# Attention products as pairs of 64-row matmuls, with separate accumulators for the two halves

## The chip, the cores and the metric

The kernel runs on one core of a Trainium2 chip. The metric is device microseconds from launch to end. TensorE (PE in the profile) multiplies, with its weight loads on a row of their own (PEld); VectorE (DVE) and ScalarE (ACT) do the elementwise work; SyncE (SP) issues the DMAs.

## What is computed

```python
scores = (1 / S) * z @ z.T            # per batch; S = 3008, z is S x 64
attn = maximum(scores, 0) ** 2
x = u * (attn @ v)                    # u, v: S x 256, two batches
h = x @ w_in                          # 256 -> 2048
x = (h - tanh(h)) @ w_out             # 2048 -> 256
out = (sigmoid(x @ w_gate) * (x @ w_val)) @ w2_out   # 256 -> 1536 -> 256
```

The reference works on two batches of 3008 tokens, attention first, then the two feed-forward networks (FFNs) on all 6016 tokens. The FFN weights are float64.

## The kernel before

A float32 operand is split into hi and lo, float32r numbers of 12 significant bits, and a product is made of three passes: hi x hi, lo x hi, hi x lo, summed in PSUM. Everything is transposed: features on partitions, tokens along the free dimension, in 12 chunks of queries, six per batch: five of 512 tokens and one of 448.

Attention takes a chunk's keys in 12 units of two 128-key tiles. `front` makes the scores of both tiles into one PSUM tile `s` of two banks (pool `psf`, two such tiles). A z tile holds hi and lo twice, so that 128 partitions are filled: its first plane is hi over lo, its second lo over hi. With the first plane as weights, the product with the first plane of the queries gives hi x hi + lo x lo, that with the second hi x lo + lo x hi: two matmuls of 128 rows for a tile, four for a unit, with a fourth product, lo x lo, among them. `mid1` is Relu and Square on ScalarE, CAST to `ah` and subtraction to `al` on VectorE. `back`, two units later, multiplies v into two accumulators, one for each 128 features (`acc0`, `acc1`): three passes, two tiles, two features, 12 matmuls. In a chunk's last unit the second key tile has only 64 keys; they stand in it twice, so that hi and lo of the scores share one pass: 10 matmuls. `end` comes one unit after the last `back` (`LATE`): two multiplies by u on VectorE, and a DMA to `spill`.

Accumulators come from the pool `psa`: tags `acc0` and `acc1` with two banks each, so four banks. A chunk takes one of each tag, and the next chunk the other.

The order of everything is written out by hand. The last loop goes over units n; in each it emits the steps in `todo` (loads, splits of z and v, one step of the float64 weights' decoding, which goes on all through attention), then `front` and `mid1` of unit n, `mid2` of unit n-1, a pending `end`, and `back` of unit n-2 (for attention). Each engine runs its own instructions in that order, and semaphores tie the engines together. The first FFN joins in the last attention chunk; until then attention has TensorE to itself.

Of the kernel before, what the change touches and what calls it, by code (L numbers as in the profile page):

```python
# [7 lines left out]
F32 = mybir.dt.float32  # L8
F32R = mybir.dt.float32r
U32 = mybir.dt.uint32  # L10
I64 = mybir.dt.int64
AF = mybir.ActivationFunctionType
ALU = mybir.AluOpType

P = 128
NQ = 512

# h - tanh(h) = tanh(h) * (GAMMA * tanh(BETA * h))^2 to 2e-6 for |h| below 0.28, where
# the square passes SQUARE_MAX; past it the difference itself is as good, and is taken.
BETA = 0.3157513921594212  # L20
GAMMA = 1.8284945624500233
SQUARE_MAX = 0.0259977

# A float64 is read as two uint32 words. Its high word, seen as a float32 and scaled by 2^-48, has the
# exponent of the wanted float32 three bits too low; these are the bounds where that exponent is in range.
WORD_MIN = 2.0**-63
WORD_MAX = 1.875 * 2.0**-32

# [2 lines left out]
def squared_relu_attention__then__two_ffns(  # L31
# [9 lines left out]
    w2_out: bass.AP,  # L41
    outT: bass.AP,
):
    """Float32 products run as float32r passes: x = hi + lo exactly, hi and lo of 12 significant
    bits each, and a @ b = a_hi b_hi + a_hi b_lo + a_lo b_hi, summed in float32 in PSUM.

    Everything is transposed: features on partitions, tokens (chunks of up to 512) along the free
    dimension. The float64 weights come as int64 and are decoded to float32 while attention runs."""
    nc = tc.nc
    B, S, D = v.shape  # L50
    DQ = zT.shape[1] // 2
    FF1 = w_in.shape[1]
    FF2 = w2_gate.shape[1]
    ND = D // P
    KT = -(-S // P)
    KP = KT // 2
    NZ = -(-S // NQ)
    HALF = S - (KT - 1) * P
    SCALE = 1.0 / S
    assert HALF * 2 == P and ND == 2 and DQ * 2 == P and KT % 4 == 0  # L60
    LATE = 1  # units from a chunk's last back to the emptying of its accumulators
    START = 2.5  # the unit of the last attention chunk after which the FFNs come in
    LAG = 5  # units that the second FFN stays behind the end of the first
    W2_LAG = 16  # units from the first FFN's start to the first split of the second's weights

    ring = ctx.enter_context(tc.tile_pool(name="ring", bufs=42))
    work = ctx.enter_context(tc.tile_pool(name="work", bufs=9))
# [1 line left out]
    psf = ctx.enter_context(tc.tile_pool(name="psf", bufs=2, space=bass.MemoryType.PSUM))  # L69
    psa = ctx.enter_context(tc.tile_pool(name="psa", bufs=2, space=bass.MemoryType.PSUM))  # L70
# [10 lines left out]
    z_t, v_t, u_t, x_t, y_t, w_t, w32 = {}, {}, {}, {}, {}, {}, {}  # L81

    chunks = []
# [3 lines left out]
    NC = len(chunks)  # L87
    spill = [nc.dram_tensor(f"x_{c}", (P, ND, chunks[c][3]), F32, kind="Internal").ap() for c in range(NC)]

# [1 line left out]
    def z_steps(b, j):  # L91
        box = []

# [37 lines left out]
        return load, lambda: split(0), lambda: split(1)  # L131

    def w_steps(src, key, g, rows):
        """Two tiles of 128 x 512 weights: float64 words to float32, kept in one slot."""
        raw, t = [], []

        def load():
            for i in range(2):
                r = slot([2, 256], I64, f"raw_{key}{g}_{i}")
                if rows:  # L140
                    s = src[(2 * g + i) * 2 * P : (2 * g + i + 1) * 2 * P]
                else:
                    s = src[:, (2 * g + i) * 256 : (2 * g + i + 1) * 256]
                nc.sync.dma_start(out=r, in_=s.rearrange("(t p) d -> p t d", p=P))
                raw.append(r)

        def words(i, h):
            return raw[i].rearrange("p t f -> p (t f)").bitcast(U32).rearrange("p (n two) -> p n two", two=2)[:, :, h]

        def magnitude():  # L150
            w = slot([2, 512], F32, f"{key}{g}_32")
            s = slot([2, 512], U32, f"{key}{g}_s")
            t.extend((w, s))
            for i in range(2):
                nc.scalar.activation(w[:, i], words(i, 1).bitcast(F32), AF.Abs, scale=2.0**-48)
            nc.vector.tensor_scalar(w, w, WORD_MAX, WORD_MIN, ALU.min, ALU.max)

        def sign():
            for i in range(2):
                nc.vector.tensor_scalar(t[1][:, i], words(i, 1), 0x80000000, None, ALU.bitwise_and)  # L160

        def join():
            w, s = t[0].bitcast(U32), t[1]
            nc.vector.scalar_tensor_tensor(
                out=w, in0=w, scalar=3, in1=s, op0=ALU.logical_shift_left, op1=ALU.bitwise_or
            )
            nc.vector.tensor_scalar(s, w, 0xFF800000, None, ALU.bitwise_and)

        def rest(i):
            s = t[1][:, i].bitcast(F32)  # L170
            nc.vector.scalar_tensor_tensor(
                out=s, in0=words(i, 0), scalar=2.0**-52, in1=s, op0=ALU.mult, op1=ALU.mult
            )

        def add():
            w, s = t[0], t[1].bitcast(F32)
            nc.vector.tensor_tensor(out=w, in0=w, in1=s, op=ALU.add)
            w32[key, g] = w

        def split(i):  # L180
            w = w32[key, g][:, i].rearrange("p (t f) -> p t f", t=2)
            r = slot([2, 2, 256], F32R, f"{key}{2 * g + i}")
            nc.scalar.copy(r[:, 0], w)
            sub(r[:, 1], w, r[:, 0])
            w_t[key, 2 * g + i] = r

        return (load, magnitude, sign, join, lambda: rest(0), lambda: rest(1), add), (
            lambda: split(0),
            lambda: split(1),
        )  # L190
# [19 lines left out]
        sub(lo[:, :, :n], x[:, :, :n], hi[:, :, :n])  # L210
        x_t[c] = (hi, lo)

# [1 line left out]
    class Unit:  # L214
        def accumulate(self, acc, wt, hl, w, first, last):
            n = self.n
# [25 lines left out]
    class Attention(Unit):  # L242
        kind, ahead = 0, 2
# [40 lines left out]
        def end(self, acc):  # L284
            u, n = u_t[self.c], self.n
            for d in range(ND):
                nc.vector.tensor_tensor(out=u[:, d, :n], in0=acc[d][:, :n], in1=u[:, d, :n], op=ALU.mult)  # L287
            nc.sync.dma_start(out=spill[self.c], in_=u[:, :, :n])

    class Ffn1(Unit):  # L290
        kind, ahead = 1, 3
# [50 lines left out]
    class Ffn2(Unit):  # L342
        kind, ahead = 2, 3
# [34 lines left out]
                copy(o[:, d, :n], acc[d][:, :n])  # L378
                nc.sync.dma_start(out=outT[d * P : (d + 1) * P, self.t0 : self.t0 + n], in_=o[:, d, :n])

# [1 line left out]
    N1, N2 = FF1 // P // 2, FF2 // P  # L382
    units = [Attention(c, i) for c in range(NC - 1) for i in range(KP)]
    n_att = len(units)
    mixed = [(i, 0, Attention(NC - 1, i)) for i in range(KP)]
    mixed += [(START + f, 1, Ffn1(0, f)) for f in range(N1)]
    mixed += [(KP + (c - 1) * N2 + f * N2 / N1, 1, Ffn1(c, f)) for c in range(1, NC) for f in range(N1)]
    mixed += [(KP + c * N2 + f + LAG, 2, Ffn2(c, f)) for c in range(NC) for f in range(N2)]
    units += [t[2] for t in sorted(mixed, key=lambda t: t[:2])]
    start, where = {}, {}  # L390
# [7 lines left out]
    def at(n, fn):  # L398
        todo.setdefault(max(n, 0), []).append(fn)

    # z and v: those of the first batch as early as it goes, those of the second while the first runs out
    for b in range(B):
        zs = [z_steps(b, j) for j in range(NZ)]
        vs = [v_steps(b, j) for j in range(NZ)]
# [1 line left out]
        if b == 0:  # L406
            early = [-2] * NZ
        else:
            early = [-2 - 2 * (NZ - j) for j in range(NZ)]
# [7 lines left out]
        for j in range(NZ):  # L417
            n = need[j] + early[j]
# [3 lines left out]
    for c in range(NC):  # L422
        at(start[0, c] + 2, lambda c=c: load_u(c))
        n = start[1, c]
# [7 lines left out]
    n = 8  # L432
    half = start[0, NZ]
    split = {}
    for k, p in enumerate(parts):
# [5 lines left out]
        if half - 14 < n < half + 4:  # L441
            n = half + 4
    for f in range(N1):
        n = where[1, 0, f]
        at(n - 3, split["wi1_", f // 2][f % 2])
        at(n - 2, split["wo1_", f // 2][f % 2])
    for f in range(N2 // 2):
        n = where[1, 0, 0] + W2_LAG + 2 * f
        assert n < where[2, 0, 2 * f]
# [6 lines left out]
    with tc.manual_schedule():  # L456
        nc.vector.memset(square_max, -SQUARE_MAX)
        nc.scalar.activation(warm, square_max, AF.Tanh)
        accs = {}
        backs = {}  # L460
        for n, u in enumerate(units):
            backs.setdefault(n + u.ahead, []).append(u)
        pending = []
        total = len(units)
        for n in range(total + 8):
            for fn in todo.pop(n, ()):
                fn()
            if n < total:
                units[n].front()
                units[n].mid1()  # L470
            if 0 <= n - 1 < total:
                units[n - 1].mid2()
            if pending and n >= pending[0][0]:
                _, u, a = pending.pop(0)
                u.end(a)
            for u in backs.pop(n, ()):
                if u.first:
                    accs[u.kind] = [psa.tile([P, NQ], F32, tag=f"acc{d}", name=f"acc{d}") for d in range(ND)]
                u.back(accs[u.kind])
                if u.last:  # L480
                    pending.append((n + LATE, u, accs[u.kind]))
        assert not todo and not pending


# ---- launch: one core; u and z transposed, z twice and its last half tile of keys repeated, the float64 weights as int64,
# the result transposed ----
# [24 lines left out]
```

## Time and profile before

| | |
|---|---|
| Three runs | 1617.8, 1619.4, 1619.55 us, median 1619.4 |
| Profiled execution, span from first to last instruction | 1618.1 us |
| PE busy, 7176 matmuls | 1605.8 us (99%) |
| PEld busy, 7176 loads | 1350.2 us (83%) |
| DVE busy | 1108.7 us (69%) |
| ACT busy | 1033.8 us (64%) |
| Attention alone on TensorE | until about 476 us |

The page gives the profiled execution by its span alone; the times of the runs are of other executions. Busy shares are means over stages. A matmul's record lasts longer than the time by which it delays the next one, so matmuls are priced by the distance of their starts. A weight load belongs to the matmul after it and runs beside the one before.

### The profile page before, as it was taken

What the parts mean: (1) busy time and instruction counts of PE and PEld (TensorE: products, weight loads), DVE (VectorE), ACT (ScalarE), POOL (GpSimd) and SP (SyncE); (2) the same over time, 40 slices, a digit from 0 to 9 for tenths busy, and PEclk for the clock granted to TensorE, in tenths of its full rate; (3) what the DMA queues carried; (4) which work ended last, traced back from release to release, by engine and by line L of the source; (5) the groups of instructions that cost most, each with busy time, mean ns of one, the idle gap of its engine ahead of it and who ended that gap; (6) DMA issues with size and microseconds to landing.
All of it is one profiled execution on the core that took longest, in us unless ns stands there. A gap on an engine that the chain in (4) does not pass through costs nothing.

```text
span 1618.1 us, 17871 instructions
## 1 busy us (share of the span) xinstructions
PE 1605.8 (99%) x7176; PEld 1350.2 (83%) x7176; DVE 1108.7 (69%) x1278; ACT 1033.8 (64%) x1232; POOL 0.2 (0%) x4
## 2 busy tenths in 40 slices
PE   8999999999999999999999999999999999999999
PEld 6888888888888878888888888888888888888888
DVE  7988888888868987665665656666565656565642
ACT  8666677666668886656665656666666656665532
POOL 0000000000000000000000000000000000000000
PEclk9999999999999999999999999999999999999999
DMA  6222214111110000000000000000000000000000
GB/s 221 79 79 78 72 52 135 61 52 62 48 38 27 1 25 0 1 27 0 27 1 25 1 27 1 0 27 1 25 1 27 1 26 1 1 25 1 13 1 25
DMA packets 28147, 53.05 MB, mean 33 GB/s; under 512 B 1952, under 2 KB 10144, under 8 KB 28064
## 3 DMA queue, kind: packets, MB, share of 16 engines
q1 hardware_dynamic: 28064, 51.91, 9.4%
q8 instruction: 56, 0.92, 0.2%
q14 instruction: 27, 0.22, 0.0%
HBM read 39.58 MB, written 12.32 MB: 32 GB/s over the span
## 4 chain that ended last, share of the span: by engine, by line
PE 98%; DVE 1%; DMA 0%; ACT 0%; issue 0%; SPq 0%; DVEq 0%
PE acc L223 51%; PE gv L235 24%; PE h L235 16%; PE s L257 8%; DMA vraw<-v 0%; DVE e L79 0%; DVE th L316 0%; DVE th L315 0%; DVE yl L79 0%; DVE u L287 0%; ACT a L263 0%; ACT th L310 0%; ACT sq L311 0%; SPq L96 0%; DVE gl L79 0%
## 5 line engine op out<-in xcount | busy, mean ns | idle before, releaser
L79 DVE TENSOR_TENSOR e<-h,th 128x1024 f32<-128x1024 f32 (+1 forms) x96 | 115.4, 1202 | 286.9 <-ACT sq L311 286.9
L223 PE MATMUL acc<-ah,v 128*128 128x512 f32 (+1 forms) x1104 | 292.5, 387 | 0.0
L223 PEld LDWEIGHTS acc<-ah,v 128*128 128x128 f32 x1104 | 208.3, 189 | 39.7 <-DVE ah L268 0.5
L263 ACT ACTIVATE a<-s 128x1024 f32<-128x1024 f32 (+1 forms) x144 | 145.5, 1010 | 149.4 <-PE s L257 149.2
L310 ACT ACTIVATE th<-h 128x1024 f32<-128x1024 f32 (+1 forms) x96 | 97.0, 1010 | 218.2 <-PE h L235 218.2
L235 PE MATMUL h<-xh,wi 128*128 128x512 f32 (+1 forms) x768 | 234.0, 386 | 1.2 <-DVE e L79 1.2
L223 PE MATMUL acc<-p,wo 128*128 128x512 f32 (+1 forms) x864 | 215.5, 386 | 0.0
L223 PE MATMUL acc<-gh,wo 128*128 128x512 f32 (+1 forms) x768 | 204.9, 386 | 0.5 <-DVE yl L79 0.4
L223 PEld LDWEIGHTS acc<-p,wo 128*128 128x128 f32 x864 | 162.3, 188 | 29.9
L79 DVE TENSOR_TENSOR al<-a,ah 128x1024 fp32r<-128x1024 f32 (+3 forms) x156 | 175.2, 1123 | 15.2 <-DVE ah L268 0.5
L360 ACT ACTIVATE sg<-gv 128x512 f32<-128x512 f32 (+1 forms) x144 | 84.5, 587 | 157.1 <-PE gv L235 157.1
L223 PE MATMUL acc<-al,v 128*128 128x512 f32 (+1 forms) x600 | 179.0, 386 | 0.0
L235 PE MATMUL gv<-yh,wg 128*128 128x512 f32 (+1 forms) x576 | 175.4, 386 | 0.0
L235 PE MATMUL gv<-yh,wv 128*128 128x512 f32 (+1 forms) x576 | 175.2, 385 | 0.0
L361 DVE TENSOR_TENSOR sg<-gv,sg 128x512 f32<-128x512 f32 (+1 forms) x144 | 98.3, 683 | 106.4 <-ACT sg L360 106.4
L235 PEld LDWEIGHTS h<-xh,wi 128*128 128x128 f32 x768 | 144.2, 188 | 28.4 <-DVE e L79 1.6
L223 PEld LDWEIGHTS acc<-gh,wo 128*128 128x128 f32 x768 | 144.2, 188 | 28.0 <-DVE yl L79 1.2
L264 ACT ACTIVATE a<-a 128x1024 f32<-128x1024 f32 (+1 forms) x144 | 150.3, 1044 | 4.6
L235 PE MATMUL h<-xl,wi 128*128 128x512 f32 (+1 forms) x384 | 148.1, 386 | 0.0
L316 DVE COPY_PREDICATED th<-m,e 128x1024 f32<-128x1024 uint32 (+1 forms) x96 | 131.6, 1371 | 9.9
L223 PEld LDWEIGHTS acc<-al,v 128*128 128x128 f32 x600 | 113.0, 188 | 21.2
L257 PE MATMUL s<-z,z 128*128 128x512 f32 (+1 forms) x480 | 127.5, 388 | 1.8 <-ACT a L263 1.8
(81 smaller groups left out, 2184.0 us busy)
## 6 DMA issues: line engine op xcount, KB each, us to landing
raw_wo<-w_out SPq DMA_DIRECT2D x14, 512.0 KB, 5.8
vraw<-v SPq DMA_DIRECT2D x10, 512.0 KB, 6.9
u<-uT SPq DMA_DIRECT2D x10, 512.0 KB, 6.7
x<-u SPq DMA_DIRECT2D x10, 512.0 KB, 3.0
xl<-x SPq DMA_DIRECT2D x10, 512.0 KB, 3.8
outT<-o SPq DMA_DIRECT2D x20, 256.0 KB, 2.1
raw_wi<-w_in SPq DMA_DIRECT2D x8, 512.0 KB, 8.1
zraw<-zT SPq DMA_DIRECT2D x12, 256.0 KB, 5.9
```

The costliest lines, as they stand in the source:

```text
L79: nc.vector.tensor_tensor(out=out, in0=a, in1=b, op=ALU.subtract)
L223: nc.tensor.matmul(acc[d][:, :n], wt[:, wi, w, d * P : (d + 1) * P], hl[ai], start=first and m == 0, stop=last and m == len(passes) - 1,)
L235: nc.tensor.matmul(ps, w[:, wi, d, fi * P : (fi + 1) * P], xs[xi][:, d, :n], start=m == 0, stop=m == len(passes) - 1)
L257: nc.tensor.matmul(self.ps[:, e, :n], k, z_t[b, self.j][:, h, :n], start=h == 0, stop=h == 1)
L263: nc.scalar.activation(s, self.ps[:, :, :n], AF.Relu, scale=SCALE)
L264: nc.scalar.activation(s, s, AF.Square)
L310: nc.scalar.activation(t, h, AF.Tanh)
L316: nc.vector.copy_predicated(t, m.bitcast(U32), e)
L360: nc.scalar.activation(s[:, :n], self.ps[:, 0, :n], AF.Sigmoid)
L361: nc.vector.tensor_tensor(out=s[:, :n], in0=self.ps[:, 1, :n], in1=s[:, :n], op=ALU.mult)
```

## The change

The first 11 chunks use a new unit, `HalfAttention`; the twelfth keeps `Attention`. Every matmul of the new unit has only 64 rows of weights and of moving data, either partitions 0 to 63 or 64 to 127, and instructions alternate between the two. In `front` the upper and lower half make the scores of the two key tiles, each with three passes and without lo x lo: six matmuls of 64 rows. In `back` each product over 128 keys is cut into its two halves of 64, which sum into accumulators of their own: 24 matmuls, 18 in the last unit. A chunk thus holds four accumulator banks. `end` follows at once after the last `back`: for each feature half ScalarE copies the second half's accumulator to SBUF, and VectorE adds the first half's to it; then one multiply by u. In a chunk's first and last unit the products are sorted by feature. Comments are removed, and nothing else is different.

```diff
+    class HalfAttention(Attention):
+        def front(self):
+            b, n = self.b, self.n
+            self.ps = psf.tile([P, 2, NQ], F32, tag="f", name="s")
+            q = z_t[b, self.j]
+            for m, (ki, qi) in enumerate(((0, 0), (1, 0), (0, 1))):
+                for e in range(2):
+                    i = 2 * self.i + e
+                    r, c = slice(e * DQ, (e + 1) * DQ), (i % 4) * P
+                    nc.tensor.matmul(
+                        self.ps[:, e, :n], z_t[b, i // 4][r, ki ^ e, c : c + P], q[r, qi ^ e, :n], start=m == 0, stop=m == 2
+                    )
+
+        def mid1(self):
...
+            nc.scalar.activation(s, self.ps[:, :, :n], AF.Relu, scale=SCALE)
+            nc.scalar.activation(s, s, AF.Square)
+            self.hl = [tmp([2, NQ], F32R, k) for k in ("ah", "al")]
+            hi, lo = (t[:, :, :n] for t in self.hl)
+            nc.vector.tensor_copy(hi, s)
+            sub(lo, s, hi)
+
+        def back(self, acc):
+            n, vt = self.n, v_t[self.b, self.i]
+
+            steps = [(h, d, e, w, a) for e in range(2) for w, a in ((0, 0), (1, 0), (0, 1)) for d in range(ND) for h in range(2)]
+            if self.first or self.last:
+                steps.sort(key=lambda t: t[1])
+            if self.last:
+
+                steps = [t for t in steps if t[2] == 0]
+                tail = [[(h, d, 1, h, 0) for h in range(2)] for d in range(ND)]
+                steps = steps[:6] + tail[0] + [(d, d, 1, 0, 1) for d in range(ND)] + steps[6:] + tail[1]
+            banks = [t[:2] for t in steps]
+            for k, (h, d, e, w, a) in enumerate(steps):
+                r = slice(h * HALF, (h + 1) * HALF)
+                nc.tensor.matmul(
+                    acc[h][d][:, :n],
+                    vt[r, w, e, d * P : (d + 1) * P],
+                    self.hl[a][r, e, :n],
+                    start=self.first and banks[k] not in banks[:k],
+                    stop=self.last and banks[k] not in banks[k + 1 :],
+                )
+
+        def end(self, acc):
+            u, n = u_t[self.c], self.n
+            other = tmp([ND, NQ], F32, "other")
+            for d in range(ND):
+                nc.scalar.copy(other[:, d, :n], acc[1][d][:, :n])
+                nc.vector.tensor_tensor(out=other[:, d, :n], in0=acc[0][d][:, :n], in1=other[:, d, :n], op=ALU.add)
+            nc.vector.tensor_tensor(out=u[:, :, :n], in0=other[:, :, :n], in1=u[:, :, :n], op=ALU.mult)
+            nc.sync.dma_start(out=spill[self.c], in_=u[:, :, :n])
...
-    units = [Attention(c, i) for c in range(NC - 1) for i in range(KP)]
+    units = [HalfAttention(c, i) for c in range(NC - 1) for i in range(KP)]
...
+                halves = isinstance(u, HalfAttention)
                 if u.first:
-                    accs[u.kind] = [psa.tile([P, NQ], F32, tag=f"acc{d}", name=f"acc{d}") for d in range(ND)]
-                u.back(accs[u.kind])
-                if u.last:
-                    pending.append((n + LATE, u, accs[u.kind]))
+                    accs[u.kind] = [
+                        [psa.tile([P, NQ], F32, tag=f"acc{d}", name=f"acc{d}") for d in range(ND)] for _ in range(1 + halves)
+                    ]
+                acc = accs[u.kind] if halves else accs[u.kind][0]
+                u.back(acc)
+                if u.last and halves:
+                    u.end(acc)
+                elif u.last:
+                    pending.append((n + LATE, u, acc))
```

VectorE's queue at the end of the third chunk, before: `ah` and `al` are hi and lo of a unit's scores, `wi1` and `wo1` FFN weights being decoded, and `u2` takes the chunk's result; an instruction's waits stand in brackets.

```order
L177 TENSOR_TENSOR wi1_2_32_1000<-wi1_2_32_1000,wi1_2_s_1001 128x1024
L268 CAST ah_1147<-a_1144 128x1024 [waits Activation_49]
L79 TENSOR_TENSOR al_1148<-a_1144,ah_1147 128x1024 [waits DVE_49,PE_49]
L156 TENSOR_SCALAR wo1_2_32_1163<-wo1_2_32_1163 128x1024 [waits Activation_49]
L268 CAST ah_1180<-a_1177 128x1024 [waits Activation_49]
L79 TENSOR_TENSOR al_1181<-a_1177,ah_1180 128x1024 [waits DVE_49,PE_49]
L287 TENSOR_TENSOR u2_833<-acc0_859,u2_833 128x512 [waits DMAHW1_49,PE_49]
L287 TENSOR_TENSOR u2_833<-acc1_860,u2_833 128x512 [waits PE_49]
```

The same place on VectorE after the change:

```order
L177 TENSOR_TENSOR wi1_2_32_1424<-wi1_2_32_1424,wi1_2_s_1425 128x1024
L314 CAST ah_1640<-a_1637 128x1024 [waits PE_49,Activation_49]
L79 TENSOR_TENSOR al_1641<-a_1637,ah_1640 128x1024 [waits DVE_49]
L344 TENSOR_TENSOR other_1662<-acc0_1199,other_1662 128x512 [waits PE_49,Activation_49]
L344 TENSOR_TENSOR other_1662<-acc1_1200,other_1662 128x512 [waits Activation_49]
L345 TENSOR_TENSOR u2_1174<-other_1662,u2_1174 128x1024 [waits DMAHW2_49,DVE_49]
L156 TENSOR_SCALAR wo1_2_32_1671<-wo1_2_32_1671 128x1024 [waits Activation_49]
L314 CAST ah_1690<-a_1687 128x1024 [waits Activation_49]
```

The reading of the accumulators has moved one unit forward; it stands behind CAST and subtraction of the unit whose front comes just before the chunk's last products.

TensorE's queue at the same boundary, before: the last value products of the third chunk (`acc0_859`, `acc1_860`), a front (`s`), the first value products of the fourth chunk (`acc0_1187`, `acc1_1188`).

```order
L223 MATMUL acc0_859<-al_1095,v0_11_426 128x512 [waits DVE_49]
L223 MATMUL acc0_859<-al_1095,v0_11_426 128x512
L223 MATMUL acc1_860<-al_1095,v0_11_426 128x512 x2
L257 MATMUL s_1172<-z0_3_212,z0_1_104 128x512 [waits Activation_49]
L257 MATMUL s_1172<-z0_3_212,z0_1_104 128x512 x3
L223 MATMUL acc0_1187<-ah_1122,v0_0_101 128x512 [waits DVE_49]
L223 MATMUL acc1_1188<-ah_1122,v0_0_101 128x512
L223 MATMUL acc0_1187<-ah_1122,v0_0_101 128x512
```

And after the change, with four accumulators for a chunk (`acc0_1199` to `acc1_1202`, then `acc0_1694` to `acc1_1697`):

```order
L331 MATMUL acc1_1200<-ah_1562,v0_11_558 128x512
L331 MATMUL acc1_1202<-ah_1562,v0_11_558 128x512
L302 MATMUL s_1680<-z0_3_246,z0_1_104 128x512 [waits Activation_49]
L302 MATMUL s_1680<-z0_3_246,z0_1_104 128x512 x5
L331 MATMUL acc0_1694<-ah_1601,v0_0_101 128x512 [waits DVE_49,Activation_49]
L331 MATMUL acc0_1696<-ah_1601,v0_0_101 128x512 [waits DVE_49]
L331 MATMUL acc0_1694<-ah_1601,v0_0_101 128x512
L331 MATMUL acc0_1696<-ah_1601,v0_0_101 128x512
```

The front has six matmuls in place of four, and the first value products of the next chunk have a wait for ScalarE and one more for VectorE.

## Rows read from the trace of the kernel before

**Rows 1.** Part 1 of the page: busy time, share of span, instructions.

```profile
PE 1605.8 (99%) x7176; PEld 1350.2 (83%) x7176; DVE 1108.7 (69%) x1278; ACT 1033.8 (64%) x1232; POOL 0.2 (0%) x4
```

**Rows 2.** Part 4 of the page: the chain that ended last, by engine and line.

```profile
PE 98%; DVE 1%; DMA 0%; ACT 0%; issue 0%; SPq 0%; DVEq 0%
PE acc L223 51%; PE gv L235 24%; PE h L235 16%; PE s L257 8%; DMA vraw<-v 0%; DVE e L79 0%; DVE th L316 0%; DVE th L315 0%; DVE yl L79 0%; DVE u L287 0%; ACT a L263 0%; ACT th L310 0%; ACT sq L311 0%; SPq L96 0%; DVE gl L79 0%
```

**Rows 3.** Busy time of each engine by window: attention, and around 585 us.

```profile
core 0: us, PE busy (x) PEld busy (x) DVE busy (x) ACT busy (x) POOL busy (x), PEclk, DMA share, GB/s
...
30.00:476.00 446.00, 446.00 (x1989) 373.22 (x1988) 368.49 (x472) 295.17 (x317) 0.00 (x0) 1.00 0.20 68
...
574.00:590.00 16.00, 14.36 (x59) 10.66 (x59) 15.21 (x18) 15.35 (x19) 0.00 (x0) 1.00 0.19 62
```

**Rows 4.** Timeline of TensorE: start, length, instruction; a later chunk, then 448 columns.

```profile
182.73 1.07 PE L257 MATMUL s<-z,z 128*128 128x512 f32 x4
...
245.05 0.97 PE L257 MATMUL s<-z,z 128*128 128x448 f32 x4
...
248.29 0.98 PE L257 MATMUL s<-z,z 128*128 128x448 f32 x4
```

**Rows 5.** Timeline of all engines at the end of the third chunk.

```profile
139.66 1.07 PE L257 MATMUL s<-z,z 128*128 128x512 f32 x4
...
140.77 1.03 ACT L263 ACTIVATE a<-s 128x1024 f32<-128x1024 f32 x1 [1.50 <-PE s L257]
...
141.83 1.06 ACT L264 ACTIVATE a<-a 128x1024 f32<-128x1024 f32 x1
142.62 0.87 PEld L257 LDWEIGHTS s<-z,z 128*128 128x128 f32 x4
...
142.84 1.07 PE L257 MATMUL s<-z,z 128*128 128x512 f32 x4
142.93 0.69 DVE L268 CAST ah<-a 128x1024 fp32r<-128x1024 f32 x1 [0.47 <-ACT a L264]
...
143.72 1.22 DVE L79 TENSOR_TENSOR al<-a,ah 128x1024 fp32r<-128x1024 f32 x1
...
144.65 0.62 PE L223 MATMUL acc<-al,v 128*128 128x512 f32 x2
144.87 0.69 DVE L156 TENSOR_SCALAR wo<-wo 128x1024 f32<-128x1024 f32 x1
...
146.47 1.07 PE L257 MATMUL s<-z,z 128*128 128x512 f32 x4
```

**Rows 6.** Groups by line and shape: count, then busy us and mean ns.

```profile
L223 PEld LDWEIGHTS acc<-ah,v 128*128 128x128 f32 x1104 | 208.3, 189 | 39.7 <-DVE ah L268 0.5
...
L79 DVE TENSOR_TENSOR yl<-acc,yh 128x512 fp32r<-128x512 f32 x20 | 12.8, 683 | 0.0
L287 DVE TENSOR_TENSOR u<-acc,u 128x512 f32<-128x512 f32 x20 | 12.8, 683 | 0.0
...
L378 ACT COPY o<-acc 128x512 f32<-128x512 f32 x20 | 10.7, 588 | 0.0
```

**Rows 7.** Timeline where TensorE had waited, in the stage where the FFNs begin.

```profile
574.29 1.28 DVE L79 TENSOR_TENSOR yl<-acc,yh 128x512 fp32r<-128x512 f32 x2
...
575.03 0.19 PEld L223 LDWEIGHTS acc<-gh,wo 128*128 128x128 f32 x1 [0.79 <-DVE yl L79]
...
585.05 0.30 PEld L235 LDWEIGHTS h<-xh,wi 128*128 128x128 f32 x2 [1.61 <-DVE e L79]
585.06 0.74 PE L235 MATMUL h<-xh,wi 128*128 128x512 f32 x2 [1.19 <-DVE e L79]
```

**Rows 8.** Timeline of TensorE: the last attention chunk's first front.

```profile
476.08 0.97 PE L257 MATMUL s<-z,z 128*128 128x448 f32 x4
```

More of the change, by code (lines that the diff above doesn't have):

```diff
@@ L288, in end @@
             nc.sync.dma_start(out=spill[self.c], in_=u[:, :, :n])
+    class HalfAttention(Attention):
[11 more added lines that the diff above has]
+        def mid1(self):
+            n = self.n
+            a = tmp([2, NQ], F32, "a")
+            s = a[:, :, :n]
+            nc.scalar.activation(s, self.ps[:, :, :n], AF.Relu, scale=SCALE)
[31 more added lines that the diff above has]
+            nc.sync.dma_start(out=spill[self.c], in_=u[:, :, :n])
```

## The prediction

> **What bounds the kernel now.** I read the page's engine table first, then the chain that ended last, then TensorE's timeline inside attention. TensorE's matmul row is busy 99% of the span [rows 1], and the chain runs over PE for 98% of it: 8% on the score products of L257, 51% on all products of L223, attention's and the FFNs' together [rows 2]. VectorE, the next, has 69% [rows 1], in attention between 30 and 476 us 368 of 446 us [rows 3]. TensorE waits nowhere in that stretch: 446.00 us busy, at a granted clock of 1.00 [rows 3]. So time here is the number of matmuls times the pitch from one matmul's start to the next, plus whatever makes TensorE wait. The pitch: the second front of one chunk starts at 139.66, that of the next at 182.73, with 190 matmuls between them, 0.2267 each; a whole unit of 448 columns takes from 245.05 to 248.29, 16 matmuls, 0.2025 each [rows 4, 5]. A matmul's own recorded length (0.39) is no price, since they overlap.
>
> **What the change removes.** A unit (two key tiles) now has 4 score and 12 value matmuls, the last unit of a chunk 4 and 10: 11 x 16 + 14 = 190 in a chunk. Afterwards it has 6 and 24 matmuls of 64 rows, the last unit 6 and 18. If two run side by side that is 15 pairs, 12 in the last unit: 11 x 15 + 12 = 177 pairs. What is saved is the score product of lo with lo, which the 128 rows compute along, one matmul in four; value products are only cut in two. Eleven chunks change: ten of 512 columns and one of 448.
>
> **What a pair costs** is the term everything hangs on, and no row of before shows a 64-row matmul. A pair needs two weight loads where a matmul needed one. A recorded load lasts 0.189 [rows 6], which would not fit twice, but that is not its pitch. Where TensorE had waited, two loads take 0.30 together, so the second starts 0.11 after the first, and the two matmuls beside them take 0.74 [rows 7] where an unhindered two take 0.62 [rows 5]: the first streams some 0.115 to 0.12 after its load starts. The lower bound of a pair is thus two loads at their pitch, 0.216 to 0.22. Its upper bound with overlap I put at 0.25: a matmul's pitch is 0.0134 longer than 512 columns at 2.4 GHz, and that gap could come two times more. Without overlap a pair is two matmuls, 0.453. I take 0.230: load, stream, load, stream strictly in turn, twice 0.115, which is nearest to the rows of a waited load and just above the pitch of one matmul. Ten chunks: 177 x 0.230 = 40.71 against 190 x 0.2267 = 43.07, -2.36 each, -23.6. The 448 chunk: loads don't shrink with the columns, 40.71 against 190 x 0.2025 = 38.48, +2.2. Together **-21.4 us**.
>
> **What it adds: a wait at every chunk's end.** Until now a chunk held two of four accumulator banks and the next took the others; the two u<-acc multiplies came a unit later and nobody waited. Now a chunk holds all four, so the next chunk's first value products wait for the ScalarE copy of one half and the VectorE add that reads the other. The order shows that add behind the CAST and subtraction of the newest unit, on VectorE's in-order queue. Worked on one boundary [rows 5]: the front starts at 139.66, Relu 140.77, Square 141.83, CAST 142.93, subtraction 143.72 to 144.94, that is 5.28 after the front's start. The front shrinks from 4 x 0.2267 = 0.91 to 0.69, plus up to 0.115 for the second half trailing: 0.10 to 0.22 earlier, I take 0.15, so 5.13. The next independent VectorE operation starts 0.07 before that recorded end (144.87): 5.06. The add is like u<-acc, 0.68 [rows 6]: 5.74. The signal takes some 0.06 (of two yl reads that begin at 574.29 the first is done 0.68 later [rows 6], 574.97, and the load waiting for it starts at 575.03 [rows 7]), and the matmul streams 0.115 after that: 5.9. TensorE stands there after front, last back and front, 3 + 9 + 3 pairs of 0.230 = 3.45, for the second half some 0.1 later, 3.55. **It waits 2.4 us.** The copies (0.59 each [rows 6]) start after Square, 3.0 after the front's start, and end by 4.2: no wait of their own. Around the 448 chunk it is less, some 2.1; at the last boundary, where the plain Attention order wants the second feature half's bank one matmul later, up to 2.8. Eleven boundaries: **+26.4** (23 to 31). It isn't made up later, for TensorE has no slack in attention. Queued behind that add are the second add, the multiply by u and a weight step; so the next unit's CAST comes some 2 us later, but its value products lie two units on.
>
> **Costs that I take as nothing.** VectorE gets one 1.2 us multiply more per chunk (two adds stand where the two multiplies stood) and loses some 0.7 in the last unit: 5 us, under a cover of 446 - 368. ScalarE gets 13 us of copies, on 295 busy of 446 [rows 3]; without that cover they cost 0.59 each. The u spill goes out some us later and is read back only in the FFN stage. At the start TensorE waits for loads and splits, so I count no gain there.
>
> **Sum.** -21.4 + 26.4 = +5.0 on the profiled span of 1618.1: 1623.1. The median of the three runs is 1.3 above that span: **1624 us**.
>
> **Rivals.**
> Loads fully hidden. If loads of the one half run while the other streams, a pair costs one matmul's pitch: 13 x 0.2267 x 10 = -29.5, the 448 chunk +0.4 (177 pairs at two loads, 0.22, against 38.5), with the boundaries -2.7: 1617. Were the gap of 0.0134 hidden as well, 0.22 a pair gives -41.3 + 0.4 + 26.4: 1605, and 0.216 gives 1598. For it: the load pitch of 0.11. Against: in the steady stream a load starts only when the matmul before its own starts (the front's loads at 142.62, its matmuls at 142.84 [rows 5]). It decides below 0.228. The Trainium skill (TensorE: Matmul & The Clock Gate, Part 3, The mechanism) has weight loads go ahead of running matmuls where the row group differs, and matmuls start and end in order; by it the time is this rival's 1617, and no run here shows it yet.
> A second gap per pair. If the 0.0134 between two matmuls stops both halves, a pair costs 0.240: ten chunks -5.9, the 448 one +4.0, with the boundaries +24.5: 1644; at 0.25 it is 1663. Each half has its own weights to change, which speaks for it; that the halves share no rows, against. It decides from 0.237. The same page of the Trainium skill (Part 3, Measured speedup vs the span model) gives four 32-row matmuls side by side 3.07 times, not 4; an estimate from that, a tenth of a matmul for each further tile, would make a pair 0.2494 and the time 1657.
> No overlap at all. The halves run one after another, 354 x 0.2267 = 80.3 in a chunk, +37.2 ten times, and 354 x 0.2025 - 38.5 = +33.2. TensorE is then later than the add at a boundary (30 x 0.2267 = 6.8 against some 6) and waits for nothing: +405, 2024. For it: nothing in the trace shows two matmuls at once. Against: the operands lie in disjoint partition halves and the results in different banks.
> The boundary wait is hidden, by another order on VectorE than the one read: -21.4, 1598. The order speaks against it.
> A fall of the clock in 2.4 us of idleness is possible too: the longest idle stretch now, 1.6 us before 585.05 [rows 7], stands in a window of granted clock 1.00 [rows 3], and nothing longer is there. It goes into the upper end of the range.
>
> **Chances.** Forecast (a pair of 0.228 to 0.236, with the wait) 0.42, its own range 1619 to 1637; hidden loads 0.27; a second gap, with the clock, 0.17; no overlap 0.11; hidden wait 0.03. A measurement of this kernel can tell about 0.2% from no change, 3.2 us. Faster, below 1616.2, are 0.23 of the hidden loads and the hidden wait: 0.26. Within it are the rest of the hidden loads and the forecast's lower end: 0.16. Slower 0.58. The range from 1602 to 1662 leaves out no overlap, some 0.04 at the bottom and 0.03 at the top.
>
> **What the changed profile would show.** A pair pitch of 0.23: fronts 3.45 apart where they are 3.63 now (142.84 to 146.47 [rows 5]). Eleven TensorE waits of about 2.4 us, released by the add of L344, on the first value products of the next chunk. The last attention chunk's first front near 481 us instead of 476.08 [rows 8]; from there on nothing should differ but the last of these waits. I am wrong if the pitch is off by more than 0.007, of which each 0.001 is 1.95 us (1947 pairs), or if the wait is not there.

## The result, and the profile after

The changed kernel takes 1628.6 us (median of four runs, 1627.5 to 1629.1) against 1618.6 for the kernel before beside it: 1.0063 times as long, 95% interval 1.0049 to 1.0077. The prediction was 1624, slower. The profiled span is 1626.3, 8.2 longer.

The page of the changed kernel, parts 1 and 4 (compare [rows 1, 2]): busy time, share and instructions; the chain by engine.

```profile
span 1626.3 us, 21466 instructions
...
PE 1596.9 (98%) x8980; PEld 1362.2 (84%) x8980; DVE 1113.3 (68%) x1256; ACT 1043.9 (64%) x1254; POOL 0.2 (0%) x4
...
PE 94%; DVE 2%; ACT 2%; issue 1%; DMA 0%; SPq 0%; DVEq 0%
```

TensorE has 1804 more matmuls and 8.9 us less busy time: the pairs do run together. But the chain (the work that ended last, followed back), 98% on PE and 1% on VectorE before, now passes through VectorE and ScalarE for 4%.

Timeline of TensorE, changed kernel, the fronts of two units of 512 columns and of two of 448 (compare [rows 4, 5]):

```profile
368.46 1.06 PE L302 MATMUL s<-z 64*128 64x512 f32 x6
...
371.87 1.06 PE L302 MATMUL s<-z 64*128 64x512 f32 x6
...
253.01 0.85 PE L302 MATMUL s<-z,z 64*128 64x448 f32 x6
...
256.05 0.92 PE L302 MATMUL s<-z,z 64*128 64x448 f32 x6
```

Fronts are 3.40 apart for 15 pairs: 0.2267 a pair, exactly the pitch of one 128-row matmul. At 448 columns it is 3.04 / 15 = 0.2027, again that of one matmul.

The end of the third chunk, all engines, the place of [rows 5]:

```profile
139.99 1.03 ACT L310 ACTIVATE a<-s 128x1024 f32<-128x1024 f32 x1 [1.28 <-PE s L302]
...
141.66 1.01 PE L302 MATMUL s<-z,z 64*128 64x512 f32 x6
142.02 1.05 ACT L343 COPY other<-acc 128x512 f32<-128x512 f32 x2
142.15 0.69 DVE L314 CAST ah<-a 128x1024 fp32r<-128x1024 f32 x1 [0.31 <-ACT a L311]
...
142.64 0.49 PE L331 MATMUL acc<-ah,v 64*128 64x512 f32 x1
142.87 1.23 DVE L79 TENSOR_TENSOR al<-a,ah 128x1024 fp32r<-128x1024 f32 x1
...
144.02 1.28 DVE L344 TENSOR_TENSOR other<-acc,other 128x512 f32<-128x512 f32 x2
...
144.76 0.73 PE L331 MATMUL acc<-ah,v 64*128 64x512 f32 x3 [1.62 <-DVE other L344]
...
146.51 1.48 PE L331 MATMUL acc<-ah,v 64*128 64x512 f32 x4
147.36 1.05 PE L331 MATMUL acc<-al,v 64*128 64x512 f32 x2
...
148.97 0.39 PE L302 MATMUL s<-z,z 64*128 64x512 f32 x1
```

One half's first value product goes at 142.64, when ScalarE has copied the bank that it takes; the other half's waits until 144.76 for the add, which stands behind CAST and subtraction. That is the predicted wait. TensorE's idle time in it is 1.62, less than the delay of 2.4, since that one product still runs; its start and the next one's are 2.12 apart. But then something follows that the sum didn't have: four matmuls, two pairs, have a record of 1.48, and the next front comes 7.31 after the last one (141.66 to 148.97) where a wait of 2.4 on top of 3.40 would make 5.8. The windows tell why (columns as in [rows 3]; the third number from the end is the granted clock):

```profile
142.87:144.76 1.89, 0.27 (x3) 0.01 (x2) 1.89 (x3) 1.89 (x4) 0.00 (x0) 1.00 0.00 0
145.43:148.84 3.41, 3.41 (x20) 2.65 (x18) 3.38 (x4) 0.77 (x1) 0.00 (x0) 0.50 0.40 154
360.00:375.00 15.00, 13.38 (x114) 10.60 (x113) 12.85 (x16) 10.05 (x12) 0.00 (x0) 1.00 0.60 211
30.00:481.00 451.00, 433.04 (x3667) 382.36 (x3665) 369.64 (x449) 300.15 (x332) 0.00 (x0) 0.97 0.21 71
```

TensorE is idle, its clock still granted in full; soon after work resumes it is granted half, 1.2 GHz, for 3.41 us. This happens at nine of the ten waits, each time for 3.41, and begins between 0.1 before work resumes and 1.2 after. The tenth wait, in the third window, is as long and no fall follows. There a boundary can be read without the fall:

```profile
359.31 1.04 PE L302 MATMUL s<-z,z 64*128 64x512 f32 x6
360.32 0.49 PE L331 MATMUL acc<-ah,v 64*128 64x512 f32 x1
362.44 0.72 PE L331 MATMUL acc<-ah,v 64*128 64x512 f32 x3 [1.62 <-DVE other L344]
...
365.06 1.06 PE L302 MATMUL s<-z,z 64*128 64x512 f32 x6
```

From 359.31 to 365.06 is 5.75: 2.35 more than 3.40. With a fall it is 7.31 at the third chunk's end, 1.56 more again.

The waits of TensorE for the adds: us of idleness in total, times, longest.

```profile
PE acc L331 <- DVE other L344: 17.8, 10, 2.7
```

Ten, not eleven: at the last boundary the first products of the plain `Attention` chunk start at once, at 492.24, before the adds at 492.77; so its two banks must be those that ScalarE's copies set free. The longest, 2.7, is where the chunk of 448 columns begins: there a weight step of 1.22 stands on VectorE ahead of CAST.

### The profile page after: what moved, and what is told of

It is laid out like the page before. It is cut to its first block, busy times and chain, and to the rows that moved or that the text cites. A ratio compares the mean times of both kernels' runs of the same rounds, so it can differ in the third digit from the quotient of the medians.

```text
span 1626.3 us, 21466 instructions
## 1 busy us (share of the span) xinstructions
PE 1596.9 (98%) x8980; PEld 1362.2 (84%) x8980; DVE 1113.3 (68%) x1256; ACT 1043.9 (64%) x1254; POOL 0.2 (0%) x4
## 4 chain that ended last, share of the span: by engine, by line
PE 94%; DVE 2%; ACT 2%; issue 1%; DMA 0%; SPq 0%; DVEq 0%
PE acc L223 29%; PE gv L235 24%; PE acc L331 21%; PE h L235 15%; PE s L302 5%; ACT a L310 1%; PE s L257 1%; DVE ah L314 1%; ACT a L311 0%; DVE other L344 0%; DMA vraw<-v 0%; ACT other L343 0%; DVE e L79 0%; DVE v L79 0%; DVE th L373 0%
## 5 line engine op out<-in xcount | busy, mean ns | idle before, releaser
L331 PE MATMUL acc<-ah,v 64*128 64x512 f32 (+1 forms) x2068 | 350.2, 398 | 18.1 <-DVE other L344 17.8
L331 PEld LDWEIGHTS acc<-ah,v 64*128 64x128 f32 x2068 | 263.3, 191 | 51.0 <-DVE other L344 20.9
L331 PE MATMUL acc<-al,v 64*128 64x512 f32 (+1 forms) x1034 | 229.7, 397 | 0.0
L310 ACT ACTIVATE a<-s 128x1024 f32<-128x1024 f32 (+1 forms) x132 | 134.5, 1019 | 147.8 <-PE s L302 141.8
L79 DVE TENSOR_TENSOR al<-a,ah 128x1024 fp32r<-128x1024 f32 (+2 forms) x145 | 173.4, 1196 | 6.0
L331 PEld LDWEIGHTS acc<-al,v 64*128 64x128 f32 x1034 | 155.4, 191 | 13.6 <-DVE al L79 0.8
L314 DVE CAST ah<-a 128x1024 fp32r<-128x1024 f32 (+1 forms) x132 | 90.5, 685 | 78.0 <-ACT a L311 78.0
L311 ACT ACTIVATE a<-a 128x1024 f32<-128x1024 f32 (+1 forms) x132 | 138.9, 1052 | 4.2
L374 DVE COPY_PREDICATED th<-m,e 128x1024 f32<-128x1024 uint32 (+1 forms) x96 | 131.6, 1371 | 10.6 <-ACT wi L183 0.5
```

The costliest lines, as they stand in the source:

```text
L79: nc.vector.tensor_tensor(out=out, in0=a, in1=b, op=ALU.subtract)
L310: nc.scalar.activation(s, self.ps[:, :, :n], AF.Relu, scale=SCALE)
L311: nc.scalar.activation(s, s, AF.Square)
L314: nc.vector.tensor_copy(hi, s)
L331: nc.tensor.matmul(acc[h][d][:, :n], vt[r, w, e, d * P : (d + 1) * P], self.hl[a][r, e, :n], start=self.first and banks[k] not in banks[:k ...
L374: nc.vector.copy_predicated(t, m.bitcast(U32), e)
```

## The experiments

My theory after the result: pairs cost one matmul's pitch, the loss is the place of the add on VectorE, and TensorE's idleness costs a second time through its clock. Rivals: the halves' clock falls because 64-row matmuls fill the array less; the need for four banks costs in any order; the gain would be had with the scores alone.

**Keep TensorE busy through the wait.** In `HalfAttention`, the score loop of `front` is made a method `scores`; ahead of ten chunks' first value products it runs three more times into the same tile:

```diff
                 units[n].front()
+                if any(isinstance(u, HalfAttention) and u.first for u in backs.get(n, ())) and units[n].kind == 0 and units[n].c:
+                    for _ in range(3):
+                        units[n].scores()
                 units[n].mid1()
```

> The changed kernel, but ahead of each of ten chunks' first value products (all boundaries but the last) TensorE makes the scores of the newest unit three more times into the same PSUM tile, 9 pairs x 0.2267 = 2.04 us of work that changes nothing. It fills the wait for the accumulators without shortening it. My theory (the wait costs some 2.1 us itself, and the idleness of TensorE makes the granted clock fall to half for 3.41 us, which costs another 1.7 in nine of the eleven boundaries): no fall at the ten boundaries, 9 x 1.7 = 15 us less than the changed kernel, about 1613. Rival (the clock falls because 64-row matmuls keep the array half as busy, or the loss is all wait): falls stay, or the time stays, 1628.

Measured: 1614.5 us, 0.9977 of the kernel before (0.9968 to 0.9986), 14.1 less than the changed kernel, with 180 matmuls more. Timeline of TensorE at the same boundary, and below it the window of attention:

```profile
138.76 3.10 PE L306 MATMUL s<-z,z 64*128 64x512 f32 x24
141.48 1.15 PE L335 MATMUL acc<-ah,v 64*128 64x512 f32 x4
...
144.53 1.06 PE L306 MATMUL s<-z,z 64*128 64x512 f32 x6
```

```profile
30.00:474.00 444.00, 442.13 (x3903) 369.55 (x3901) 375.74 (x455) 307.36 (x340) 0.00 (x0) 1.00 0.21 72
```

The boundary takes 5.77 (138.76 to 144.53), as the one without a fall did, and the granted clock is 1.00 throughout. So the wait itself costs 2.4 and the falls together 14, some 1.57 each; more 64-row matmuls took the falls away, so the clock doesn't fall because of the 64 rows.

**The same wait with 128-row matmuls.** Two attempts on the kernel before. In the first, two accumulator tiles are allocated and left unused ahead of a chunk's, and `end` follows at once:

```diff
                 if u.first:
+                    if u.kind == 0 and 0 < u.c < NC - 1:
+                        for d in range(ND):
+                            psa.tile([P, NQ], F32, tag=f"acc{d}", name=f"skip{d}")
...
-                if u.last:
+                if u.last and u.kind == 0 and u.c < NC - 1:
+                    u.end(accs[u.kind])
+                elif u.last:
```

> The kernel before, all products at 128 rows, but chunks two to eleven use the same two accumulator banks as the chunk ahead of them, and those chunks' end comes at once after their last products: at ten boundaries the next chunk waits for the two multiplies by u, which stand behind the newest unit's CAST and subtraction. The wait, from the rows of before: subtraction done 5.28 after the front's start, multiply 0.68, signal and stream 0.17, against 18 x 0.2267 = 4.08 when TensorE arrives: about 2.0 us each, +20. My theory (TensorE's idleness alone makes the granted clock fall, by chance of when it comes): falls to half of 3.41 us at some of the ten waits, 1.7 each: 1618 + 20 + 2 to 17 = 1640 to 1655. Rival (the falls belong to 64-row matmuls): no fall, 1638.

Measured: 1616.9 us, 0.999 of the kernel before (0.9981 to 1.0). The edit didn't make what it was meant to: no wait of TensorE for the multiplies came, so the chunks must have gone on alternating, and an unused tile holds no bank. It says nothing on the clock, but it shows that the early `end`, behind the same CAST and subtraction, costs nothing as long as TensorE need not wait for its banks.

The second attempt lets eleven chunks write the very same tiles (with the early `end` as above):

```diff
                 if u.first:
-                    accs[u.kind] = [psa.tile([P, NQ], F32, tag=f"acc{d}", name=f"acc{d}") for d in range(ND)]
+                    if u.kind or u.c in (0, NC - 1):
+                        accs[u.kind] = [psa.tile([P, NQ], F32, tag=f"acc{d}", name=f"acc{d}") for d in range(ND)]
```

> As in e5, but the eleven chunks write the very same accumulator tiles, so that the wait is there: the first value product of chunks two to eleven waits for the first multiply by u, the second for the second. From rows of before: subtraction done 5.28 after the front's start, multiply 0.68, signal and stream 0.17, 6.1 against 18 x 0.2267 = 4.08 when TensorE arrives: 2.0 us, and some 0.4 more for the second feature half, 2.4 at each of ten boundaries, +24. My theory (idleness of TensorE by itself makes the granted clock fall to half for 3.41 us, by chance of when it comes): falls at some of the ten, 1.7 each: 1644 to 1659. Rival (the falls belong to 64-row matmuls): no fall, 1642.

Measured: 1652.8 us, 1.0212 of the kernel before (1.0195 to 1.0229). The waits of TensorE, the timeline at one boundary, and the window after it:

```profile
PE acc L223 <- DVE u L287: 19.0, 10, 3.0
```

```profile
101.68 1.28 DVE L287 TENSOR_TENSOR u<-acc,u 128x512 f32<-128x512 f32 x2
...
102.42 1.55 PE L223 MATMUL acc<-ah,v 128*128 128x512 f32 x4 [1.70 <-DVE u L287]
...
104.54 1.91 PE L223 MATMUL acc<-ah,v 128*128 128x512 f32 x4
```

```profile
103.94:107.35 3.41, 3.41 (x10) 2.63 (x9) 2.12 (x4) 0.00 (x0) 0.00 (x0) 0.50 0.96 288
```

Ten waits, and the same stretches of 3.41 us at half the clock after six of them, with no 64-row matmul before them. The forecast 24 for the waits and 6 x 1.6 for the falls make 34, the whole loss. So idleness by itself, 1.7 us here, can be followed by a fall. Whether a given one is stays open: nine of ten were in the changed kernel, six of ten here, four of ten in the next but one experiment, nearly all with 2.1 us from the start of the matmul before the wait to that of the one after.

**Let the adds go first.** TensorE's order is untouched; on ScalarE the copies stand ahead of the newest unit's Square, on VectorE the adds ahead of its CAST and subtraction, and the multiply by u behind them. `mid1` is cut into `relu` and `rest`, `end` into `end` and `store`:

```diff
-                units[n].mid1()
+                ends = [u for u in backs.get(n, ()) if isinstance(u, HalfAttention) and u.last]
+                if ends:
+                    backs[n] = [u for u in backs[n] if u not in ends]
+                    units[n].relu()
+                    for u in ends:
+                        u.back(accs[u.kind])
+                        u.end(accs[u.kind])
+                    units[n].rest()
+                    for u in ends:
+                        u.store()
+                else:
+                    units[n].mid1()
```

> The changed kernel, but at a chunk's end the copies and adds that read the accumulators stand ahead of the newest unit's Square, CAST and subtraction in ScalarE's and VectorE's queues; TensorE's order is the same. My theory (pairs cost one matmul's pitch, 0.2267, so the products gain 32 us, and all the loss is the place of the adds): add of the first feature half done some 3.35 us after the front's start where TensorE arrives at 3.4 to 3.5, waits below 0.3 each, no clock falls, 1618.6 - 32 + 3 = 1590. Rival (the loss at a boundary is the need for all four banks as such, whatever the order): waits of 1 us or more stay and the time is above 1605.

Measured: 1592.7 us, **0.9844 of the kernel before** (0.9827 to 0.986), and faster than both. Timeline at the third chunk's end, and the window of attention:

```profile
136.67 1.06 PE L309 MATMUL s<-z,z 64*128 64x512 f32 x6
136.81 0.68 DVE L353 TENSOR_TENSOR other<-acc,other 128x512 f32<-128x512 f32 x1
...
137.35 0.92 PE L340 MATMUL acc<-ah,v 64*128 64x512 f32 x4
...
137.71 0.69 DVE L353 TENSOR_TENSOR other<-acc,other 128x512 f32<-128x512 f32 x1 [0.22 <-ACT other L352]
...
138.67 0.69 DVE L323 CAST ah<-a 128x1024 fp32r<-128x1024 f32 x1 [0.27 <-ACT a L320]
...
140.17 1.06 PE L309 MATMUL s<-z,z 64*128 64x512 f32 x6
```

```profile
30.00:453.00 423.00, 421.12 (x3740) 388.26 (x3738) 374.45 (x457) 308.00 (x342) 0.00 (x0) 1.00 0.22 75
```

The first add ends at 137.49, just when the matmul that needs it comes; front to front is 3.50, 0.10 over the steady 3.40. CAST now comes after the adds, and TensorE doesn't wait for it. Only two waits of TensorE for the adds are left (below), at the first chunk's end and where the 448 one begins; there a weight step of 1.22 on VectorE holds up the adds until 0.9 and 1.6 after the front's start, against 0.14 here. I had expected waits below 0.3 at every boundary. No fall follows. So four banks are no loss by themselves.

```profile
PE acc L340 <- DVE other L353: 1.9, 2, 1.3
```

**Break the alternation.** In ten of a chunk's units the value products run one half first, then the other:

```diff
             if self.first or self.last:
                 steps.sort(key=lambda t: t[1])
+            else:
+                steps.sort(key=lambda t: t[0])
```

> The changed kernel, but in ten of a chunk's twelve units the 24 value products run all 12 of the lower half first and then all 12 of the upper. My theory (two 64-row matmuls run side by side only if they follow each other in the queue on different halves): these 110 units lose nearly all overlap in back, 11.5 x 0.2267 = 2.6 us each, +287, about 1910, less where a longer unit hides the boundary waits. Rival (the halves overlap whatever the order, or 64-row matmuls are simply twice as fast): 1628.

Measured: 1757.5 us in one run, 129 more than the changed kernel, less than half of what was expected. A unit takes 4.62 instead of 3.40, so 5.4 pitches are lost where 11.5 were expected. Timeline of TensorE over one unit:

```profile
129.89 1.07 PE L333 MATMUL acc<-ah,v 64*128 64x512 f32 x4
130.79 0.61 PE L333 MATMUL acc<-al,v 64*128 64x512 f32 x2
131.25 1.18 PE L333 MATMUL acc<-ah,v 64*128 64x512 f32 x6
132.15 0.39 PE L333 MATMUL acc<-al,v 64*128 64x512 f32 x1
132.27 0.39 PE L333 MATMUL acc<-ah,v 64*128 64x512 f32 x1
132.38 0.39 PE L333 MATMUL acc<-al,v 64*128 64x512 f32 x1
...
133.67 0.50 PE L302 MATMUL s<-z 64*128 64x512 f32 x1
133.89 0.39 PE L333 MATMUL acc<-ah,v 64*128 64x512 f32 x1
134.01 0.39 PE L302 MATMUL s<-z 64*128 64x512 f32 x1
```

Each half's program is `ah` four times, `al` twice, and again. The first nine starts are one half's, a pitch apart, alone. Then `ah` and `al` mix: the other half's first `ah` has started while the first half still had its last `ah` and its two `al` to start. Likewise the next front's score products (133.67) start between the last value products, which stand ahead of them in the queue. The rows carry no half; I tell them apart by that program, which the order of `ah` and `al` fits. So two matmuls side by side need different halves, as I held; but the queue isn't strictly in turn: one for an idle half starts before some three earlier ones for the busy half. TensorE thus doesn't run quite in the order written. The Trainium skill (TensorE: Matmul & The Clock Gate, Part 3, The mechanism) has starts strictly in program order; here the measurement differs.

**The scores alone.** In the kernel before, only `front` is that of `HalfAttention`; value products, banks and `end` stay:

```diff
-    units = [Attention(c, i) for c in range(NC - 1) for i in range(KP)]
+    units = [HalfScores(c, i) for c in range(NC - 1) for i in range(KP)]
```

> The kernel before with the scores alone as 64-row pairs (six matmuls, lo x lo left out as in the changed kernel); value products at 128 rows, two accumulator banks and the late end as before. So no boundary waits. If changing between 64 and 128 rows costs nothing: one matmul less in each of 132 units, 120 x 0.2267 + 12 x 0.2026 = 29.6 less, 1589. If TensorE runs empty at each of the 264 changes, by some 0.16 (the 0.39 of a matmul's record less its pitch): +42, 1631. I expect something between, nearer to the second, since the Trainium skill (TensorEngine Tiling (Array Packing), Key Properties) says that a change of mode drains the engine.

Measured: 1646.0 us, 1.0174 of the kernel before (1.0159 to 1.019), and above the 1631 that I had put as the upper end. Timeline of TensorE:

```profile
119.92 0.97 PE L299 MATMUL s<-z,z 64*128 64x512 f32 x6
120.82 1.20 PE L223 MATMUL acc<-ah,v 128*128 128x512 f32 x4
...
123.76 0.96 PE L299 MATMUL s<-z,z 64*128 64x512 f32 x6
```

A unit takes 3.84 (119.92 to 123.76), 0.44 more than 15 pitches. Three pairs take 0.90 to the next product instead of 0.68. So a change between 64 and 128 rows costs some 0.22 us, twice a unit (0.20 in the 448 chunk, where a unit takes 3.44): the saved matmul, 0.2267, is paid back twofold. The page of the Trainium skill on TensorEngine Tiling (Array Packing), Key Properties, says that a change of mode drains the engine; the trace agrees in so far as each change costs, with 0.22 as the price, more than the 0.16 that I had worked out for a TensorE that runs empty. This is why the value products are better halved with the scores, though halving gains them nothing. The changed kernel pays it five times where its 64-row units meet the plain ones, some 1.1 us.

## Why the prediction was right, and where it wasn't

The sign and the range held; of the three terms behind them one was right, one wrong and one missing. That the total came within 5 us of 1624 is luck: the products gained 10.6 more than forecast, and the clock, which was in no sum, took 14.1.

- **The pair's pitch** was mis-sized: 0.2267, not 0.230, and 0.2027 at 448 columns, not 0.230. The product term is 10 x (177 x 0.2267 - 43.07) + 177 x 0.2027 - 38.5 = -32.0, not -21.4. This is the rival of hidden loads, which I gave 0.27. What failed is the choice of "load, stream, load, stream in turn". Its lower bound fell too: two loads at 0.11 in turn would not fit into 0.2027. The row of weight loads after a wait, below, shows why: three loads take 0.29, where two in turn took 0.30 in [rows 7], so two of the three start together. The loads of the two halves don't share a pitch. The rule of the Trainium skill that I cited for that rival, loads ahead of running matmuls of the other row group, agrees with the pair's pitch of 0.2267.

```profile
144.75 0.29 PEld L331 LDWEIGHTS acc<-ah,v 64*128 64x128 f32 x3 [1.93 <-DVE other L344]
```

- **The wait** was right in place, cause and size: 2.35 against 2.4 (359.31 to 365.06). Ten instead of eleven; the supposed 2.8 at the last boundary was nothing. Around the 448 chunk it was not less, as supposed, but more: 3.3 where it begins and 2.5 where it ends. The boundaries of the busy-wait kernel, less a normal unit each, sum to 25, against 26.4.
- **The clock** was named but left without a price or a sum, as a part of the upper end. It costs 14.1 (changed kernel less busy-wait kernel), nine times 1.57. That is less than half of 3.41, since at half the clock a pair takes 0.427 (two take 0.85, from 146.51 to 147.36), not twice 0.2267; 3.41 x (1 - 0.2267 / 0.427) is 1.60. The row that I leaned on was misread: the 1.61 without a fall in [rows 7] is the idleness of the weight loads, and the matmuls' own is 1.19, against 1.62 here.
- **Covers** held: VectorE is busy 369.64 of 451 us in attention, ScalarE 300.15, and no boundary wait of TensorE was for a late CAST.
- The **changes of mode** at the last boundary, 1.1 us, weren't in the sum.

Sum: -32.0 + 25.1 + 14.1 + 1.1 = +8.3, and the span grew by 8.2. So close a match is partly chance, for the start, which no term holds, differs by more: the fourth front begins at 16.36 after the change and at 17.24 before. The front that I put near 481 comes at 484.08:

```profile
484.08 1.08 PE L257 MATMUL s<-z,z 128*128 128x448 f32 x4
```

Of the other rivals, no overlap, a second gap and a wait hidden by another order than the one read are refuted for the kernel as changed; the last became true when the order was changed.

What stays open: why a fall follows one wait and not another of the same length.

## What to carry to other kernels

A float32r matmul whose contraction is cut into halves on disjoint partitions cost nothing more here when the halves alternated in the queue, so products that only fill up 128 rows can be left out; but the matmuls around them had better be of the same row count, for each change cost 0.22 us. When a change takes all accumulator banks, whatever reads the old ones is suddenly on the critical path: put it ahead of other work in its engine's queue, here two copies and two adds, which turned +0.6% into -1.6%. And price a TensorE wait of 2 us at more than its length: in two of three kernels most such waits were followed by a fall of the clock, some 1.6 us more each.

## What the runs showed of the hardware that I had not expected

- Two 64-row matmuls of float32r side by side take one matmul's time, weight loads of both included: 0.2267 at 512 columns, 0.2027 at 448.
- Thirty waits with 1.9 to 3.4 us between two matmul starts, most of them 2.1 with 1.6 to 1.7 idle, were followed by 3.41 us at half the clock in 19 cases, with 64-row and with 128-row matmuls. At half the clock a 512-column matmul or pair takes 0.427, not twice 0.2267.
- A matmul for an idle half starts ahead of some three that stand before it in the queue for the busy half.
